# A list scheduler with other durations and loads, one choice for 20 units, and a first weight load behind the gathers, in a gated linear attention with a routed FFN

## The chip, the cores and the metric

One core of one Trainium2 chip. The metric is the device time of the whole kernel in microseconds (us). Before: 425.37 us, the median of 3 runs (424.46 to 426.98).

## The reference

Two stages, on one core, in float32:

```python
# attention: batch 4, 8 heads, 768 tokens, head size 48
for t in range(S):
    state = alpha[:, :, t, :, None] * state + np.einsum('bhd,bhe->bhde', k[:, :, t], v[:, :, t])
    y[:, :, t] = np.einsum('bhd,bhde->bhe', q[:, :, t], state)
...
# routed FFN: x is y laid out as 3072 tokens x 384, 8 experts, w1 384x1024, w2 1024x384
logits = x @ w_gate
order = np.argsort(-flat)            # all 3072*8 logits, largest first
for idx in order:
    tok, e = (int(idx) // E, int(idx) % E)
    if assigned[tok] >= 0 or counts[e] >= cap:   # cap = 384
        continue
    assigned[tok] = e
...
out[mask] = np.maximum(x[mask] @ w1[e], 0.0) @ w2[e]
```

So every token goes to one expert, each expert gets exactly 384 tokens, and who gets which depends on one global order of the logits.

## The kernel before

**Attention.** The sequence is cut into 6 chunks of 128 tokens; a unit is one chunk of one batch, all 8 heads, so there are 24 units (`unit(n)`, L352). A unit runs over all five engines:

- DVE: a scan over alpha (`sc`, L363), a reciprocal (L365), the keys scaled by it (`kh`, L373), a second scan (`ga`, L368), and the update of the carried state (`st`, L420 and L426).
- POOL: the queries scaled (`qh`, L378), the causal mask on the scores (`sm`, L407, two per unit), the carried state scaled (`ms`, L423).
- PE: transposed keys (L391), scores (L401), the state's increment (L415), outputs (L434: a part from the carried state, `qh` by `ms`, then a part from the chunk, `sm` by `vr`), the gate's logits (L457) and their transpose into one PSUM bank (L462, `lg`).
- ACT: evictions of PSUM (L394, L405, L451, L461).
- SP: the loads of alpha, k, q, v (L332).

**Choice.** `choice` (L468) takes the logits of a group of finished units. On DVE it copies them out of PSUM (L481), takes each token's largest logit (L484), turns it into digits (L490 to L107), marks the chosen expert (L498 to L502) and compares the first digit with 128 thresholds (`cmp`, L506, 128 elements per unit and partition). PE then counts per expert and threshold, one matmul per unit (L518). DVE adds the counts up (L529) and after the last group but one takes `need` (L534). In this kernel there are four groups: units 0 to 7, 8 to 15, 16 to 19, 20 to 23, each due as soon as its units are done (`at = n1 + 0.6`).

**Routing and FFN.** For each expert in turn, `round_` (L710) finds the threshold logit, digit by digit: five `level`s (L672), each a group of PE counts (L682), a row sum (L687), a DVE maximum (L690), then a compare on DVE (L699). Then it computes the indices of the 384 tokens (L834). Tokens are gathered from DRAM (`x_dram`, three indirect DMAs on POOL, L841), transposed (L913) and split in a high and a low part. An expert's weights come in `GP` = 4 pieces of 768 KB. Each piece is loaded once by POOL's queue (`hi`, L862), ACT writes its negative (two instructions, L872), and a second, accumulating DMA adds the full-precision weights to leave the remainder (`low`, L876). The FFN needs both: `ffn1` (L946) multiplies high by high, high by low and low by high, ACT and DVE split the hidden layer (L957, L959), `ffn2` (L977) does the second product, and the rows are scattered to the output (L991). Between attention and FFN the attention output, which lies transposed in SBUF, is transposed back and stored to `x_dram` (SP, L547, 24 stores): 8 units in the attention's own list, 16 after it (`rest`, L621).

**What sets the order.** Neither part is emitted as it is written. `op(...)` (L173) notes an operation with its engine, a duration in us, what it reads and writes, the PSUM banks it uses (`take`/`give` hold one for a chain of operations) and `at`, the time at which it is due. `plan()` (L193) is a list scheduler: it simulates the engines with these durations, and on each engine takes, of the operations that could start within 0.12 us of the earliest, the one with the smallest key:

```python
for o in reversed(ops):
    o.key = min([o.at] + [s.key for s in succ[o]])
...
t, o = min(((t, o) for t, o in c if t <= t0 + 0.12), key=lambda z: (z[1].key - z[1].boost, z[1].idx))
```

What comes out is the fixed order of the instructions on each engine; on the chip every engine works its own list off in order and waits where an input isn't there. There are two plans: one for attention with the choices (L580) and one for routing and FFN (L1020). `FIRST_HI` says how many `hi` pieces of expert 0, expert 1 and the others are issued as soon as the expert's number is known (L893); the others follow the gathers in `second` (L884).

Of the kernel before, what the change touches and what calls it, by code (L numbers as in the profile page):

```python
# [29 lines left out]
def gla_moe_kernel(ctx, tc, q, k, v, alpha, w_gate, w12, out):  # L30
# [4 lines left out]
    HP = H // 2  # L35
# [137 lines left out]
    def op(eng, dur, fn, r=(), w=(), banks=(), at=0.0, after=(), lat=LAT, take=None, give=None, follow=(), boost=0.0,  # L173
           dma=0.0, soft=(), small=False):
        o = Op()
        o.small = small
# [12 lines left out]
        o.pre = pre  # L189
        ops.append(o)  # L190
        return o

    def plan(begin=()):  # L193
# [7 lines left out]
        queue, again = {}, {}  # L201
        after_small = False
        todo = list(ops)
        out_ = []
        while todo:
# [121 lines left out]
    for i, (e, d_, f) in enumerate(LATE):  # L327
        lates.append(op(e, d_, f, after=lates[-1:], at=9.0 + 0.5 * i))


    def loads(n):
        r = RING  # L332
        sz = 1.25
        first = n == 0
        for nm, src, dst in (("al", alpha, AL), ("k", k, KR), ("q", q, QR), ("v", v, VR)):
            def fn(nm=nm, src=src, dst=dst):
                t = dst[n % r[nm]]
                if nm != "al":
# [7 lines left out]
            op("SP", sz if nm != "v" else 0.95, fn, w=[(nm, n)], at=n - 3.0, lat=2.2)  # L346


    def unit(n):
# [9 lines left out]
        for i, (lo, hi) in enumerate(parts):  # L359
# [23 lines left out]
            op("DVE", 1.26 / f, fore, r=[("al", n), ("sc", n)], w=[("ga", n)], at=n)  # L383
            op("DVE" if n == 0 else "POOL", 1.0 / f, scale_q, r=[("q", n), ("ga", n)], w=[("qh", n)], at=n + 0.1)
        if mid:
            t = [None]

            def keys():
                t[0] = xt([128, HP, C], 0)
                for p in range(HP):  # L390
                    P_.transpose(t[0][:, p], kh[:, p], ident)  # L391

            op("PE", 0.62, keys, r=[("kh", n)], w=[("T", n)], banks=("T",), at=n + 0.2, take="T")
            op("ACT", 0.6, lambda: A.activation(kn, t[0], AF.Copy), r=[("T", n)], w=[("kn", n)],  # L394
               banks=("T",), at=n + 0.3, give="T")
# [6 lines left out]

        op("PE", 1.15, scores, r=[("kh", n), ("qh", n)], w=[("S0", n), ("S1", n)], banks=("S0", "S1"), at=n + 0.3)
        for h in range(2):
            op("ACT", 0.6, lambda h=h: A.activation(sm[:, h], sps[:, h], AF.Copy), r=[(f"S{h}", n)],  # L405
               w=[("sm", n)], banks=(f"S{h}",), at=n + 0.4)
            op("POOL", 0.95, lambda h=h: G.affine_select(  # L407
                sm[:, h], sm[:, h], pattern=[[0, HP], [1, C]], compare_op=OP.is_ge, fill=0.0, base=0,
                channel_multiplier=-1), r=[("sm", n)], w=[("sm", n)], at=n + 0.5)
        if mid:  # L410
# [6 lines left out]

            op("PE", 0.62, states, r=[("kn", n), ("v", n), ("pads", 0)], w=[("KV", n)], banks=("KX",), at=n + 0.6)
            if c == 0:
                op("DVE", 0.3, lambda: V.tensor_copy(st_, kvp), r=[("KV", n)], w=[("st", n)], banks=("KX",),  # L420
                   at=n + 0.6)
        if c:
            op("POOL", 0.42, lambda: G.tensor_tensor(ms, st_, bc(total, D), op=OP.mult),  # L423
               r=[("sc", n), ("st", n - NBAT)], w=[("m", n)], at=n + 0.15)
# [3 lines left out]

        def outputs():
            fresh = set()  # L430

            def go(h, p, lhs, rhs, last):
                g, s = p % 2, p // 2
                P_.matmul(yv[64 * g:64 * g + D, h, s], lhs, rhs, start=(h, g) not in fresh, stop=last and s == 1,  # L434
                          skip_group_check=True)
                fresh.add((h, g))

            if c:
                for p in range(HP):
                    for h in range(2):  # L440
                        hs = slice(64 * h, 64 * h + D)
                        go(h, p, ms[hs, p], qh[hs, p], False)
# [4 lines left out]
        op("PE", (0.65 if c else 0) + 1.15, outputs,  # L447
           r=[("qh", n), ("v", n), ("sm", n), ("pads", 0)] + ([("m", n)] if c else []), w=[("Y", n)],
           banks=("Y",), at=n + 0.8)
        yt = YT[n]  # L450
        op("ACT", 0.62, lambda: A.activation(yt, yv, AF.Copy), r=[("Y", n)], w=[("yt", n)], banks=("Y",), at=n + 0.9)  # L451

        def logits():
# [5 lines left out]
        lt = LT[n % RING["lt"]]  # L459
        op("PE", 0.4, logits, r=[("yt", n), ("wg", 0)], w=[("LT", n)], banks=("KX",), at=n + 1.0)  # L460
        op("ACT", 0.3, lambda: A.activation(lt, ltp, AF.Copy), r=[("LT", n)], w=[("lt", n)], banks=("KX",), at=n + 1.0)  # L461
        op("PE", 0.25, lambda: P_.matmul(lgp[:, n % 8], lt, sel, start=True, stop=True), r=[("lt", n)],  # L462
           w=[("LG", n)], banks=("KX",), at=n + 1.1, after=lg_read.get(n // 8 - 1, ()))
# [5 lines left out]
    def choice(i, n0, n1):  # L469
        sl = slice(n0, n1)  # L470
        m_ = n1 - n0
        lw = L[:, sl]
        at = n1 + 0.6 if n1 < NU else NU - 0.2
        tl = {}

        def tile_(nm, shape, dt=F32):
            tl[nm] = ap_.tile(shape, dt, name=f"{nm}_{i}")
            return tl[nm]

        def c0():  # L480
            V.tensor_copy(lw, lgp[:, n0 % 8:n0 % 8 + m_])  # L481

# [37 lines left out]

        x = op("PE", 0.06 * m_ + 0.1, counts, after=[x], banks=("KX",), at=at)

# [13 lines left out]

    done = []
    GROUPS = ((0, 8), (8, 16), (16, 20), (20, 24))

# [9 lines left out]
    for n in range(NU):  # L549
        loads(n)  # L550
        unit(n)
        for i, (n0, n1) in enumerate(GROUPS):
            if n1 == n + 1:
                choice(i, n0, n1)
    ev = []
    for n in range(Y_IN_ATTENTION):
# [9 lines left out]
        if wide:  # L566
            xo = op("PE", 0.31, lambda tr=tr: tr(0), r=[("yt", n)], after=lastw["sm", NU - 1], banks=("S0", "S1"),
                    at=40.0 + n, take=f"s{wide}")
            xo = op("PE", 0.31, lambda tr=tr: tr(1), after=[xo], banks=("S0", "S1"), at=40.0 + n)
            ev.append(op("ACT", 0.6, lambda n=n, t=t: y_evict(n, t[0]), after=[xo], banks=("S0", "S1"),  # L570
                         at=40.0 + n, give=f"s{wide}"))
        else:
            xo = op("PE", 0.31, lambda tr=tr: tr(0), r=[("yt", n)], after=lastw["S0", Y_FROM], banks=("T",),
                    at=40.0 + n, take="T")
            xo = op("PE", 0.31, lambda tr=tr: tr(1), after=[xo], banks=("T",), at=40.0 + n)
            ev.append(op("ACT", 0.6, lambda n=n, t=t: y_evict(n, t[0]), after=[xo], banks=("T",), at=40.0 + n,
# [494 lines left out]
```

## Time and profile before

| | |
|---|---|
| median of 3 runs | 425.37 us (424.46 to 426.98) |
| profiled execution | 424.8 us, its span 423.2 us, mean granted TensorE clock 0.953 |
| PE busy | 388.3 us (92% of the span), 4166 matmuls |
| DVE busy | 266.8 us (63%) |
| POOL busy | 186.5 us (44%) |
| ACT busy | 173.9 us (41%) |
| DMA | 88.85 MB, 210 GB/s over the span |
| attention, until its last `lg` | 128 us |
| routing of expert 0, gathers, first weights | 128 to 168 us |
| FFN with the other experts' routing beside it | from 163.5 us to the end |

PE is busy nearly all the time, but a busy share of 92% is a mean over three stages. The time is lost where PE is idle or runs at a lower granted clock, and that is in the first 190 us. An engine's order is fixed, so an idle PE waits for one named instruction. "PEclk" is the granted TensorE clock: 1.0 is 2.4 GHz, 0.5 is 1.2 GHz, and a mean between them is a stretch that has some of each.

### The profile page before, as it was taken

How to read it: one execution, taken by the hardware profiler on the slowest of the kernel's cores; microseconds unless marked ns; L12 is line 12 of the kernel's file. 1: busy time of each engine (PE TensorE's matmuls, PEld its weight loads, DVE VectorE, ACT ScalarE, POOL GpSimd, SP SyncE). 2: the span in 40 equal slices, each digit the busy share in tenths (PEclk: the TensorE clock that was granted, in tenths of full speed). 3: DMA queues.
4: the chain of work that ended last, by engine and by line, in shares of the span. 5: the costliest groups of instructions: out<-in, count | busy, mean ns of one | idle time of the engine just before them, and what ended most of it. 6: DMA issues, size and time to landing. Idle time of an engine off the chain costs nothing.

```text
span 423.2 us, 10477 instructions
## 1 busy us (share of the span) xinstructions
PE 388.3 (92%) x4166; PEld 343.5 (81%) x4166; DVE 266.8 (63%) x673; ACT 173.9 (41%) x320; POOL 186.5 (44%) x271
## 2 busy tenths in 40 slices
PE   6789979998888858999999999999999999999991
PEld 3667768787666846898998999999999999999990
DVE  8798898879915746686685866766766754131110
ACT  4355535554535412434326263263262263453210
POOL 9667648785810033151454372352253283430302
PEclk8699989999989688899999999999999999999997
DMA  7986756663015559999899999899899899999201
GB/s 224 390 305 211 225 166 213 203 219 103 5 37 191 172 164 249 218 263 226 219 289 265 228 354 192 198 315 189 190 324 181 171 377 196 293 298 199 79 2 57
DMA packets 30178, 88.85 MB, mean 210 GB/s; under 512 B 4144, under 2 KB 10544, under 8 KB 30128
## 3 DMA queue, kind: packets, MB, share of 16 engines
q0 software_dynamic: 12288, 59.78, 55.4%
q1 hardware_dynamic: 17840, 28.39, 20.2%
q8 instruction: 33, 0.54, 0.5%
q14 instruction: 17, 0.14, 0.1%
HBM read 78.72 MB, written 9.44 MB: 208 GB/s over the span
## 4 chain that ended last, share of the span: by engine, by line
PE 66%; DVE 13%; issue 8%; POOL 5%; DMA 5%; ACT 1%; POOLq 0%; DVEq 0%; ACTq 0%
PE h L946 19%; PE y L977 18%; PE y L434 6%; PE xt L682 6%; DMA wset<-in_w_dram 5%; PE s L401 4%; PE xt L391 2%; PE xt L913 2%; PE xt L457 2%; DVE sc L363 2%; PE xt L415 2%; POOL out_dram L991 1%; DVE kh L373 1%; DVE ga L368 1%; PE xt L830 1%
## 5 line engine op out<-in xcount | busy, mean ns | idle before, releaser
L977 PE MATMUL y<-wset,hh 128*128 128x384 f32 x384 | 101.9, 346 | 0.0
L946 PE MATMUL h<-xh,wset 128*128 128x384 f32 x384 | 91.1, 346 | 2.1 <-DMA wset<-in_w_dram 1.9
L957 ACT ACTIVATE hh<-h 128x384 fp32r<-128x384 f32 x64 | 31.2, 488 | 111.8 <-PE h L946 101.8
L959 DVE SCALAR_TENSOR_TENSOR hl<-h,hh 128x384 fp32r<-128x384 f32 x64 | 35.5, 554 | 61.2 <-ACT hh L957 61.1
L946 PEld LDWEIGHTS h<-xh,wset 128*128 128x128 f32 x384 | 68.1, 191 | 3.3 <-DMA wset<-in_w_dram 2.4
L977 PEld LDWEIGHTS y<-wset,hh 128*128 128x128 f32 x384 | 67.2, 189 | 0.0
L977 PE MATMUL y<-wset,hl 128*128 128x384 f32 x192 | 64.7, 337 | 0.0
L872 ACT ACTIVATE wset<-wset 128x768 fp32r<-128x768 f32 x64 | 51.2, 839 | 25.9 <-DMA wset<-in_w_dram 25.8
L862 POOL DMA_DIRECT2D wset<-in_w_dram x32 | 22.2, 720 | 82.8 <-DVE m L749 34.8
L876 POOL DMA_DIRECT2D wset<-in_w_dram x32 | 30.5, 1167 | 34.1 <-ACT wset L872 33.3
L946 PE MATMUL h<-xl,wset 128*128 128x384 f32 x192 | 45.2, 343 | 0.0
L841 POOL DMA_INDIRECT xr<-x_dram,idx x24 | 25.2, 1049 | 37.6 <-DVE idx L834 15.3
L991 POOL DMA_INDIRECT out_dram<-yo,idx x24 | 26.2, 1090 | 35.2 <-ACT yo L985 29.3
L407 POOL TENSOR_SCALAR_AFFINE_SELECT sm<-sm 128x512 f32<-128x512 f32 x48 | 31.1, 668 | 19.6 <-ACT sm L405 11.8
L682 PEld LDWEIGHTS <-cmp 128*128 128x128 bf16 x816 | 30.2, 118 | 8.5 <-DVE cmp L699 4.4
L378 POOL TENSOR_TENSOR qh<-qr,ga 128x512 f32<-128x512 f32 x23 | 32.0, 1391 | 10.4 <-DVE ga L368 7.8
L977 PEld LDWEIGHTS y<-wset,hl 128*128 128x128 f32 x192 | 36.0, 188 | 0.0
L405 ACT ACTIVATE sm<-s 128x512 f32<-128x512 f32 x48 | 26.7, 596 | 18.6 <-PE s L401 17.7
L946 PEld LDWEIGHTS h<-xl,wset 128*128 128x128 f32 x192 | 33.7, 189 | 0.2
L699 DVE TENSOR_TENSOR cmp<-nd,iota 128x1536 bf16<-128x1536 bf16 (+2 forms) x32 | 32.7, 1032 | 0.9
L368 DVE TENSOR_TENSOR_SCAN ga<-al,d 128x516 f32<-128x516 f32 (+1 forms) x25 | 29.6, 1184 | 2.0
L434 PE MATMUL y<-sm,vr 128*48 128x128 f32 x384 | 28.0, 292 | 2.8 <-POOL sm L407 2.8
(161 smaller groups left out, 598.0 us busy)
## 6 DMA issues: line engine op xcount, KB each, us to landing
wset<-in_w_dram POOLq DMA_DIRECT2D x64, 768.0 KB, 9.1
kr<-in_k_dram SPq DMA_DIRECT2D x24, 256.0 KB, 4.4
qr<-in_q_dram SPq DMA_DIRECT2D x24, 256.0 KB, 4.4
al<-in_alpha_dram SPq DMA_DIRECT2D x23, 258.5 KB, 3.9
vr<-in_v_dram SPq DMA_DIRECT2D x24, 192.0 KB, 3.6
x_dram<-xga SPq DMA_DIRECT2D x24, 192.0 KB, 1.9
xr<-x_dram,idx POOLq DMA_INDIRECT x24, 4.7
out_dram<-yo,idx POOLq DMA_INDIRECT x24, 6.2
```

What stands on the lines that cost most here:

```text
L368: V.tensor_tensor_scan(ga[:, lo:hi], a[:, lo:hi], dps[:, lo:hi], 1.0, op0=OP.mult, op1=OP.add)
L378: (V if n == 0 else G).tensor_mul(qh[:, ps_], qr[:, ps_], ga[:, lo:hi].rearrange("p (g x) -> p g x", x=C1)[:, :, 1:])
L407: op("POOL", 0.95, lambda h=h: G.affine_select(sm[:, h], sm[:, h], pattern=[[0, HP], [1, C]], compare_op=OP.is_ge, fill=0.0, base=0, chann ...
L434: P_.matmul(yv[64 * g:64 * g + D, h, s], lhs, rhs, start=(h, g) not in fresh, stop=last and s == 1, skip_group_check=True)
L682: P_.matmul(rt_c, cmp_[:, j // U, :, j % U], o[:, j], start=j == 0, stop=j == NU - 1, skip_group_check=True)
L699: x = op("DVE", (1.75 if nt == 128 else 0.95) / n + 0.03, lambda js=js: V.tensor_tensor(words(cbuf[t % 2], nt, js), keyed(d, nt, js), each ...
L872: pre.append(op("ACT", 0.84, lambda hs=hs: A.activation(WS[i % 2][:, 1, g][:, hs], WS[i % 2][:, 0, g][:, hs].bitcast(F32), AF.Copy, scale= ...
L876: accs[i, g] = op("POOL", 0.92, lambda: nc.gpsimd.dma_start(WS[i % 2][:, 1, g], w12.bitcast(F32R)[bass.ds(eng_reg[i], 1), :, g].rearrange( ...
L946: P_.matmul(o, WS[i % 2][:, a, g, c0 + d * 128:c0 + (d + 1) * 128], x[:, d], start=m_ == 0 and d == 0, stop=m_ == 2 and d == DB - 1)
L957: a_ = op("ACT", 0.49, lambda: A.activation(HHT[m], o, AF.Relu), after=[y], r=[("hb", n_)], w=[("hh", n_)], at=at, boost=25, lat=0.1)
L959: op("DVE", 0.54, lambda: V.scalar_tensor_tensor(HLT[m], o, 0.0, HHT[m], op0=OP.max, op1=OP.subtract), after=[a_], r=[("hb", n_), ("hh", n ...
L977: P_.matmul(YB[b][:, :Dm], a[:, bs], w, start=q == 0 and n == 0, stop=q == FB - 1 and n == 2)
```

## The change

1. **Durations and shapes in the attention's plan.** Many durations are other numbers (scores 1.15 to 0.9, key transposes 0.62 to 0.44, masks 0.95 to 0.65, `qh` 1.0 to 1.3, loads 1.25 to 0.9). Each PE operation carries a shape; a change of shape costs 0.13 or 0.2 us in the plan, and the same shape as the one before is preferred by 0.4. The outputs become two operations (`carried_` and `within`) that hold the bank Y together. Four DVE constants (`LATE`, the tables `iotas` for the digits 2 to 5) are due at 40.0, so behind everything else, in place of 16.5 to 18. Back-transposes (Y) of units 0 to 2 use the bank of the key transposes and have no lower limit (`Y_FROM` gone, `Y_WIDE` 5 to 3).
2. **One choice for 20 units.** `GROUPS` has two entries, and the first is due at `CHOICE` = 23.15. The copies of the logits out of PSUM stay apart (`logits_out`, four groups as before).
3. **First weights behind the gathers.** `FIRST_HI` for expert 0 is 0 and `second(0)` issues all four pieces behind the three gathers.

```diff
-Y_WIDE = 5
-Y_FROM = 19
+Y_WIDE = 3
+SAME, CHOICE = 0.4, 23.15
...
-FIRST_HI = (1, 2, 4)
+FIRST_HI = (0, 2, 4)
...
-                t, o = min(((t, o) for t, o in c if t <= t0 + 0.12), key=lambda z: (z[1].key - z[1].boost, z[1].idx))
+                t, o = min(((t, o) for t, o in c if t <= t0 + 0.12), key=lambda z: (
+                    z[1].key - z[1].boost - SAME * (z[1].shape == last_shape is not None), z[1].idx))
...
+                o.dur += (0.13 if o.shape != 64 else 0.2) * (o.shape != last_shape)
+                last_shape = o.shape
...
-        lates.append(op(e, d_, f, after=lates[-1:], at=9.0 + 0.5 * i))
+        lates.append(op(e, d_, f, after=lates[-1:], at=9.0 + 0.5 * i if e == "POOL" else 40.0))
...
-        sz = 1.25
+        sz = 0.9
...
-        op("PE", 1.15, scores, r=[("kh", n), ("qh", n)], w=[("S0", n), ("S1", n)], banks=("S0", "S1"), at=n + 0.3)
+        op("PE", 0.9, scores, shape=64, r=[("kh", n), ("qh", n)], w=[("S0", n), ("S1", n)], banks=("S0", "S1"), at=n + 0.3)
...
-        at = n1 + 0.6 if n1 < NU else NU - 0.2
+        at = CHOICE if n1 < NU else NU - 0.2
...
-    GROUPS = ((0, 8), (8, 16), (16, 20), (20, 24))
+    GROUPS = ((0, 20), (20, 24))
+
+    def logits_out(n0, n1):
+        x = op("DVE", 0.18, lambda: V.tensor_copy(L[:, n0:n1], lgp[:, n0 % 8:n0 % 8 + n1 - n0]),
+               r=[("LG", n) for n in range(n0, n1)], banks=("KX",), at=n1 + 0.1, after=inits + copied[-1:])
+        lg_read[n0 // 8] = lg_read.get(n0 // 8, ()) + (x,)
+        copied.append(x)
...
-            for g in range(1, GP):
+            for g in range(GP):
                 hi(g, [x], rows)
-                low(g - 1, [his[0, g]])
-                rows = [accs[0, g - 1]]
+                rows = [his[0, g]]
+                if g:
+                    low(g - 1, rows)
+                    rows = [accs[0, g - 1]]
```

Two places in the order of the instructions. The first is DVE at the end of attention; `kh` is the scaled key of unit 23, `m` to `cmp` are the choice, L the logits' copy. Before:

```order
L368 SCALAR_TENSOR_TENSOR ga_143<-al_121,d 128x516
L481 COPY L<-xt_168 128x32
L484 TENSOR_REDUCE m_2_1544<-L 128x4
L487 TENSOR_TENSOR val_2_1547<-L,m_2_1544 128x32
...
L502 TENSOR_TENSOR o_100<-ramp_b,chu_99 128x32
L506 TENSOR_TENSOR cmp_2_1584<-dig_98,iota 128x512
L373 TENSOR_TENSOR kh_146<-kr_126,sc_141 128x512
L529 TENSOR_TENSOR cnt<-cnt,xt_168 128x8
L534 TENSOR_SCALAR need<-cnt 128x8
L481 COPY L<-xt_168 128x32
```

and now:

```order
L371 SCALAR_TENSOR_TENSOR ga_143<-al_121,d 128x516
L429 TENSOR_TENSOR st_160<-ms_155,xt_168 128x192
L376 TENSOR_TENSOR kh_146<-kr_126,sc_141 128x512
L544 COPY L<-xt_168 128x32
L487 TENSOR_REDUCE m_0_1499<-L 128x20
L490 TENSOR_TENSOR val_0_1502<-L,m_0_1499 128x160
...
L505 TENSOR_TENSOR o_100<-ramp_b,chu_99 128x160
L509 TENSOR_TENSOR cmp_0_1540<-dig_98,iota 128x2560
L530 COPY cnt<-xt_168 128x8
```

The last `kh` stood behind a choice of 4 units and stands ahead of one of 20. The choices of units 0 to 7 and 8 to 15, which stood between the scans of units 10 and 11 and of units 19 and 20, are gone from there. The four `iotas` have moved: three stood behind the scan of unit 1 and one behind that of unit 2, and now they stand behind the scans of units 20, 21 and 23. On PE, the 20 counts of the new choice stand behind the `lg` of unit 21; between the `lg` of unit 19 (the last logits that the choice needs) and the counts PE has two whole units of scores, logits, outputs and `lg`.

The second place is POOL from the first expert's number (`ei`) on; `wset` is a weight piece, L862 and L875 load high parts, L876 and L889 accumulate low ones, wset_1746 and wset_1709 are expert 0's, wset_2190 and wset_2154 expert 1's. Before:

```order
L857 TENSOR_LOAD ei_1762
...
L862 DMA wset_1746<-in_w_dram 128x1536
L841 DMA xr_1747<-x_dram,idx_1825 128x384 x3
...
L862 DMA wset_1746<-in_w_dram 128x1536
...
L876 DMA wset_1746<-in_w_dram 128x1536
...
L857 TENSOR_LOAD ei_1763
```

and now:

```order
L870 TENSOR_LOAD ei_1725
...
L854 DMA xr_1710<-x_dram,idx_1788 128x384 x3
...
L875 DMA wset_1709<-in_w_dram 128x1536
...
L875 DMA wset_1709<-in_w_dram 128x1536
...
L889 DMA wset_1709<-in_w_dram 128x1536
...
L870 TENSOR_LOAD ei_1726
...
L875 DMA wset_2154<-in_w_dram 128x1536
...
L889 DMA wset_1709<-in_w_dram 128x1536
```

The first `hi` has moved from ahead of the three gathers to behind them, and expert 1's first `hi` (wset_2154) now stands ahead of expert 0's third and fourth `low`, where both of its first pieces stood ahead of the fourth `low` alone.

## Rows read from the trace of the kernel before

**Rows 1.** The page: 40 slices of granted TensorE clock, in tenths.
```profile
PEclk8699989999989688899999999999999999999997
```
**Rows 2.** Busy time by stretch: PE, PEld, DVE, ACT, POOL (count), PEclk, DMA share, GB/s.
```profile
58.00:63.00 5.00, 5.00 (x60) 4.06 (x59) 4.89 (x8) 1.19 (x2) 2.06 (x2) 0.66 0.47 151
63.00:99.00 36.00, 36.00 (x644) 28.33 (x641) 30.52 (x51) 20.19 (x42) 26.15 (x32) 1.00 0.69 220
117.00:121.00 4.00, 3.70 (x46) 2.76 (x46) 1.08 (x4) 0.00 (x0) 0.00 (x0) 0.57 0.00 0
191.00:386.00 195.00, 194.74 (x1709) 183.85 (x1710) 117.85 (x353) 81.83 (x141) 78.28 (x105) 1.00 0.97 249
```
**Rows 3.** Timeline around the first choice: start, us, engine, line, operation [idle before].
```profile
53.38 0.22 DVE L481 COPY L<-xt 128x64 f32<-128x64 f32 x1
56.91 0.68 DVE L506 TENSOR_TENSOR cmp<-dig,iota 128x1024 bf16<-128x1024 bf16 x1
55.85 0.39 PE L462 MATMUL xt<-sel,lt 128*128 128x8 f32 x2 [0.56 <-ACT lt L461]
57.91 0.40 PE L518 MATMUL xt<-o,cmp 128*128 128x8 bf16 x8 [1.67 <-DVE st L426]
```
**Rows 4.** Timeline of PE around the second choice.
```profile
104.49 0.56 PE L415 MATMUL xt<-vr,kn 128*48 128x48 f32 x16 [1.04 <-ACT yta L451]
104.99 1.16 PE L401 MATMUL s<-qh,kh 64*128 64x128 f32 x16
108.03 0.39 PE L462 MATMUL xt<-sel,lt 128*128 128x8 f32 x2
```
**Rows 5.** Timeline around the third choice, PE and DVE, and the last `lg`.
```profile
113.52 0.43 PE L457 MATMUL xt<-yta,wg 128*32 128x128 f32 x8 [0.64 <-DVE L L481]
117.16 0.68 DVE L373 TENSOR_TENSOR kh<-kr,sc 128x512 f32<-128x512 f32 x1
117.30 0.30 PE L518 MATMUL xt<-o,cmp 128*128 128x8 bf16 x4 [1.44 <-DVE cmp L506]
128.23 0.39 PE L462 MATMUL xt<-sel,lt 128*128 128x8 f32 x2
```
**Rows 6.** Timeline of DVE in the routing: the same instruction on 24 units.
```profile
149.41 0.35 DVE L766 TENSOR_TENSOR val<-L,m 128x192 bf16<-128x192 f32 x1
```
**Rows 7.** Groups of lines, 0 to 120 us: count | busy us, mean ns | idle before.
```profile
L321 DVE TENSOR_SCALAR iota<-iota 128x256 bf16<-128x256 bf16 (+1 forms) x4 | 2.6, 680 | 0.0
```
**Rows 8.** Waits, 0 to 120 us: who waited for whom: us, times, longest us.
```profile
PE xt L391 <- DVE kh L373: 2.7, 4, 1.6
```
**Rows 9.** Timeline of DVE and POOL around the first gathers.
```profile
149.68 0.15 DVE L834 TENSOR_SCALAR idx<-xt 128x3 int32<-128x3 f32 x1
146.18 0.76 POOL L862 DMA_DIRECT2D wset<-in_w_dram  x1 [21.55 <-DMA x_dram<-xga]
154.70 1.06 POOL L841 DMA_INDIRECT xr<-x_dram,idx  x1 [7.76 <-DVE g L685]
158.29 0.61 POOL L862 DMA_DIRECT2D wset<-in_w_dram  x1
```
**Rows 10.** One tile: stores to `x_dram`, 120 to 165 us.
```profile
DMA to landing us min/median/max: 1.8/1.9/6.0
```
**Rows 11.** One line: the `hi` loads (L862), 140 to 200 us.
```profile
DMA to landing us min/median/max: 6.0/8.6/14.6
```
**Rows 12.** The chain of waits, two of its DMAs: start, us, what.
```profile
158.86 9.22 DMA wset<-in_w_dram
179.86 10.97 DMA wset<-in_w_dram
```
**Rows 13.** Timeline of PE: the FFN's first matmuls, and a wait for weights.
```profile
163.52 0.76 PE L946 MATMUL h<-xh,wset 128*128 128x384 f32 x3
168.13 2.05 PE L946 MATMUL h<-xh,wset 128*128 128x384 f32 x6 [1.33 <-DMA wset<-in_w_dram]
```
**Rows 14.** The page: the costliest group of ACT's copies for the low parts.
```profile
L872 ACT ACTIVATE wset<-wset 128x768 fp32r<-128x768 f32 x64 | 51.2, 839 | 25.9 <-DMA wset<-in_w_dram 25.8
```

More of the change, by code (lines that the diff above doesn't have):

```diff
@@ L173, in op @@
     def op(eng, dur, fn, r=(), w=(), banks=(), at=0.0, after=(), lat=LAT, take=None, give=None, follow=(), boost=0.0,
-           dma=0.0, soft=(), small=False):
+           dma=0.0, soft=(), small=False, shape=None):
         o = Op()
-        o.small = small
+        o.small, o.shape = small, shape
         o.take, o.give, o.follow, o.boost, o.dma, o.soft = take, give, follow, boost, dma, soft
@@ L383, in unit @@
             op("DVE", 1.26 / f, fore, r=[("al", n), ("sc", n)], w=[("ga", n)], at=n)
-            op("DVE" if n == 0 else "POOL", 1.0 / f, scale_q, r=[("q", n), ("ga", n)], w=[("qh", n)], at=n + 0.1)
+            op("DVE" if n == 0 else "POOL", 1.3 / f, scale_q, r=[("q", n), ("ga", n)], w=[("qh", n)], at=n + 0.1)
         if mid:
@@ L391, in keys @@
                     P_.transpose(t[0][:, p], kh[:, p], ident)
-            op("PE", 0.62, keys, r=[("kh", n)], w=[("T", n)], banks=("T",), at=n + 0.2, take="T")
+            op("PE", 0.44, keys, shape=128, r=[("kh", n)], w=[("T", n)], banks=("T",), at=n + 0.2, take="T")
             op("ACT", 0.6, lambda: A.activation(kn, t[0], AF.Copy), r=[("T", n)], w=[("kn", n)],
@@ L427, in unit, with carried_, go, within @@
                    w=[("st", n)], banks=("KX",), at=n + 0.6)
[L429 to L442, printed above, removed]
+        fresh = set()
+        def carried_():
+            for p in range(HP):
+                for h in range(2):
+                    hs = slice(64 * h, 64 * h + D)
+                    go(h, p, ms[hs, p], qh[hs, p], False)
+        def go(h, p, lhs, rhs, last):
+            g, s = p % 2, p // 2
+            P_.matmul(yv[64 * g:64 * g + D, h, s], lhs, rhs, start=(h, g) not in fresh, stop=last and s == 1,
+                      skip_group_check=True)
+            fresh.add((h, g))
+        def within():
             for h in range(2):
@@ L445, in outputs @@
                     go(h, p, vr[:, 4 * (p // 2) + 2 * h + p % 2], sm[:, h, p], True)
-        op("PE", (0.65 if c else 0) + 1.15, outputs,
-           r=[("qh", n), ("v", n), ("sm", n), ("pads", 0)] + ([("m", n)] if c else []), w=[("Y", n)],
-           banks=("Y",), at=n + 0.8)
+        if c:
+            op("PE", 0.45, carried_, shape=4848, r=[("qh", n), ("m", n), ("pads", 0)], w=[("Y", n)], banks=("Y",),
+               at=n + 0.75, take="Y")
+        op("PE", 0.9, within, shape=48, r=[("v", n), ("sm", n), ("pads", 0)] + ([("Y", n)] if c else []),
+           w=[("Y", n)], banks=("Y",), at=n + 0.8, take=None if c else "Y")
         yt = YT[n]
-        op("ACT", 0.62, lambda: A.activation(yt, yv, AF.Copy), r=[("Y", n)], w=[("yt", n)], banks=("Y",), at=n + 0.9)
+        op("ACT", 0.62, lambda: A.activation(yt, yv, AF.Copy), r=[("Y", n)], w=[("yt", n)], banks=("Y",), at=n + 0.9, give="Y")
         def logits():
@@ L459, in unit @@
         lt = LT[n % RING["lt"]]
-        op("PE", 0.4, logits, r=[("yt", n), ("wg", 0)], w=[("LT", n)], banks=("KX",), at=n + 1.0)
+        op("PE", 0.23, logits, shape=32, r=[("yt", n), ("wg", 0)], w=[("LT", n)], banks=("KX",), at=n + 1.0)
         op("ACT", 0.3, lambda: A.activation(lt, ltp, AF.Copy), r=[("LT", n)], w=[("lt", n)], banks=("KX",), at=n + 1.0)
-        op("PE", 0.25, lambda: P_.matmul(lgp[:, n % 8], lt, sel, start=True, stop=True), r=[("lt", n)],
+        op("PE", 0.15, shape=128, fn=lambda: P_.matmul(lgp[:, n % 8], lt, sel, start=True, stop=True), r=[("lt", n)],
            w=[("LG", n)], banks=("KX",), at=n + 1.1, after=lg_read.get(n // 8 - 1, ()))
@@ L506, in c7 @@
             V.tensor_tensor(CM[i], keyed(dig0[:, 0], T, sl), each(iota, T, sl), op=OP.is_ge)
-        x = op("DVE", 0.18, c0, r=[("LG", n) for n in range(n0, n1)], banks=("KX",), at=at, after=inits)
-        lg_read[n0 // 8] = lg_read.get(n0 // 8, ()) + (x,)
-        for d_, f in ((0.18, c1), (0.45, c2), (0.32, c3), (0.5, c4), (0.6, c5), (0.2, c6), (0.13 * m_, c7)):
+        x = copied[-1]
+        for d_, f in ((0.1 + 0.01 * m_, c1), (0.1 + 0.01 * m_, c2), (0.3, c3), (0.5 + 0.01 * m_, c4), (0.35 + 0.01 * m_, c5),
+                      (0.15 + 0.006 * m_, c6), (0.04 + 0.073 * m_, c7)):
             x = op("DVE", d_, f, after=[x], at=at)
@@ L519, in counts @@
                           skip_group_check=True)
-        x = op("PE", 0.06 * m_ + 0.1, counts, after=[x], banks=("KX",), at=at)
+        x = op("PE", 0.034 * m_, counts, shape=128, after=[x], banks=("KX",), at=at)
         def add():
@@ L551, in gla_moe_kernel @@
         unit(n)
+        for n0, n1 in ((0, 8), (8, 16), (16, 20), (20, 24)):
+            if n1 == n + 1:
+                logits_out(n0, n1)
         for i, (n0, n1) in enumerate(GROUPS):
```

22 lines of the change are left out of this document (10 added, 12 removed).

## Prediction

> **What bounds the kernel now.** I read the page first. Its row of granted clock [rows 1] stands near full almost everywhere, with dips in the slices around 60, 120, 140 and 160 us (a slice is 10.6 us). So PE is the engine to watch, and the losses have places. The busy times by stretch [rows 2] say what these places are. From 63 to 99 us, in the middle of attention, PE is busy 36.00 of 36.00 us at clock 1.00: there PE itself is the bound, and nothing that the other engines do costs anything. From 191 to 386 us the FFN is busy 194.74 of 195.00 us at 1.00: there too. Whatever this change gains must therefore come from before 63 us, from 99 to 128 us, or from 128 to 191 us.
>
> The timeline shows who holds PE up in these stretches. In the first [rows 3], DVE takes the choice of units 0 to 7 from 53.38 us, with its own `kh` queued behind. PE waits 0.56 us at 55.85 (ACT could not evict while the copy had the bank) and 1.67 us at 57.91. That second wait is put down to `st`, but it stands at the counts, and the `cmp` in front of it ended only at 57.6. Behind these gaps the clock is 0.66 from 58 to 63 us [rows 2]. The second choice shows the same less strongly: 1.04 us at 104.49 [rows 4]. The third is worst [rows 5]: 0.64 us at 113.52, 1.44 us at 117.30 for the counts, and `kh` of unit 23 could only run at 117.16, behind the choice. The clock behind it is 0.57 from 117 to 121 us [rows 2]. The last `lg` of attention starts at 128.23.
>
> After attention, the indices of the first gather are ready at 149.83, but POOL issues it at 154.70 [rows 9]. What lies between are stores to `x_dram`: normally they land after 1.9 us, the slowest after 6.0 [rows 10]. The first weight load was issued at 146.18, among the last stores.
>
> **The sum.** It is made against the profiled execution, 424.8 us; the median of the runs is 0.6 above it, and I add that at the end.
>
> *Choices in the middle of attention, gone or moved.* A gap counts whole, since PE is the bound around it; a stretch of lower clock counts as its length times what is missing from 1.00.
> - First choice: 0.56 + 1.67 [rows 3] + 5.00 x (1 - 0.66) = 1.7 [rows 2]: -3.9 us.
> - Second choice: -1.0 us [rows 4].
> - Third choice: 0.64 + 1.44 [rows 5] + 4.00 x (1 - 0.57) = 1.7 [rows 2]: -3.8 us.
>
> Together -8.7 us. The copies of the logits stay, 0.22 us each [rows 3], and the PE counts stay in number; both are paid now.
>
> *The choice of 20 at the end.* DVE works the choice of 8 units from 53.38 to 56.91 in eleven small instructions, 3.53 us, then `cmp`, 0.68 us for 1024 elements [rows 3]. For 20 units `cmp` has 2560: 1.7 us. The small ones I leave as they are, because the same `val` instruction on 24 units takes 0.35 us [rows 6]: they are fixed cost. So 5.2 us. What hides it is PE's work between the `lg` of unit 19 and the counts, two units of scores, logits, outputs and `lg`; one unit is 3.4 us (104.99 to the end of the `lg` at 108.42, [rows 4]), so 6.8 us. The four `iotas`, 2.6 us in all [rows 7], now stand in front of it on DVE, and 5.2 + 2.6 = 7.8 us would show by 1.0; if DVE leads PE there, by nothing. I take +0.5. If only one unit of cover is left, 7.8 - 3.4 = 4.4 us are uncovered, and the lower clock behind a gap, 1.7 as above, comes on top. Bounds: 0 to +6.1.
>
> *The `iotas` leave the start.* Their 2.6 us [rows 7] stood behind the scans of units 1 and 2, with `kh` of the next unit queued after them. PE waited for `kh` 2.7 us in 4 waits, the longest 1.6 [rows 8]. I take that one wait as theirs, -1.5. Bounds: 0 (the loads are the limit there) to -2.6.
>
> *Durations, shapes, separate outputs, loads, early Y of unit 0.* These only reorder. PE's groups change shape 141 times in attention where it was 145. The trace has no price for a change; the small `lg` group, two matmuls of 8 columns, takes 0.39 us with everything in it [rows 4], so four changes are worth 0 to -1.6. Where PE is full the order of full groups changes nothing: I take 0. The transposes of unit 0 are moved, not added.
>
> *First weights behind the gathers.* Without the load among them I expect the last stores to land like the others, 6.0 - 1.9 = 4.1 us earlier [rows 10], so the gathers go at 150.6, soon after the indices (149.83). What do the weights do? The first `hi` is then issued where the second was, 158.29 - 4.1 = 154.2 [rows 9], and with the shortest landing of such a load, 6.0 us [rows 11], it is there at 160.2, ahead of the FFN's first matmul at 163.52 [rows 13]. But the stream is what ends this stage. The chain goes through the first `low`, 9.22 us from 158.86, for which PE waits 1.33 us, and through the last, 10.97 us from 179.86 [rows 12, 13]; from 191 us PE does not stop. From 158.29 to 190.83 the queue lands the same nine pieces, 3.6 us each, and now it has to land the first `hi` in the same stretch as well: -4.1 + 3.6 = -0.5 us. I take that. Bounds: -3.3 if the FFN can start as soon as its first `hi` is there (160.2 for 163.52). On the other side the first `low` must wait for that `hi` and ACT's two copies of 0.84 us [rows 14], 160.2 + 1.7 = 161.9, where it was issued at 158.86: +3.0.
>
> The Trainium skill speaks against this part: its page DMA: Bandwidth & Descriptors, section Rules for kernel authors, says to issue a DMA early, compute, and wait for it late. Rows 9 and 10 show the other side, an early load with six-microsecond stores beside it; by the rule alone this part would be worth the +3.0 of rival 2. The same page's section Anatomy of one DMA gives 2.0 us plus bytes by 436 GB/s, an estimate of 3.8 us for 768 KB, and by it this term would be 2.2 us lower; no load here came under 6.0 [rows 11], and the row decides.
>
> Sum: -8.7 + 0.5 - 1.5 - 0.5 = -10.2 us, so 414.6 for a profiled execution, and with 0.6 a median of **415.2 us**. All bounds at their best: -8.7 - 2.6 - 1.6 - 3.3 = -16.2, 409.2 us. All at their worst: -8.7 + 6.1 + 3.0 = +0.4, 425.8 us.
>
> **Rivals.**
>
> 1. *The choice of 20 isn't covered.* PE works in order, so logits and outputs of units 22 and 23 queue behind the 20 counts, and everything after attention behind those. For it: in the third choice just this wait of PE for `cmp` is there [rows 5]. Against it: that choice stood ahead of the last `kh`, this one stands behind it. Price: +6.1 for +0.5: 420.8 us.
> 2. *The first expert's weights are late.* The `hi` stands behind the gathers, the `low` behind it, and expert 1's first piece ahead of the third `low`. For it: PE already waits for the first `low` [rows 13], so any delay of it shows. Against it: the gathers come 4.1 us earlier. Price: +3.0 for -0.5: 418.7 us.
> 3. *Slower: the new order has a hole, and the clock stays down.* The plan is built on other durations, so a bank held too long or an input that comes late by the chip's time makes gaps in each unit. Behind the gaps of rows 3 and 5 the clock went towards its 1.2 GHz level. A unit's 3.4 us of work [rows 4] then takes another 3.4. It decides from four units on: 415.2 + 4 x 3.4 = 428.8 us, slower than before. Against it: in the full stretch of rows 2 there was slack on every other engine (DVE busy 30.5 of 36, POOL 26.2).
> 4. *Nothing is gained.* The choice's gaps go, but PE had to wait there for scans or loads in any case, and the waits appear elsewhere: 425.4 us. Against it: from 63 us on PE was full without any choice beside it [rows 2].
>
> **How the numbers follow.** Forecast 0.60, rival 1 0.15, rival 2 0.13, rival 3 0.06, rival 4 0.06. A measurement of this kernel can tell about 0.5% from no change, 2.1 us (its three runs spread over 2.5). The forecast and rivals 1 and 2 lie beyond that: faster 0.88, same 0.06 (rival 4), slower 0.06 (rival 3). The range runs from 409.5, nearly all bounds at their best, to 421.5, just beyond rival 1; what it leaves out is rivals 3 and 4 and sums of rivals 1 and 2.
>
> **What would show it.** In the changed profile: PE without gaps of over 0.5 us between 50 and 118 us, clock 1.00 from 58 to 63 us and at 100 to 118; the last `lg` about 10 us earlier, near 118; a wait of at most 1 us at the counts of 20; slowest store to `x_dram` near 2 us, first gather within 1 us of its indices; the first `low` still what PE waits for, about 10 us earlier than 168.1. It would be wrong if the last `lg` came at 122 or later (rival 1, or 3 with low clock over many slices), or if attention gained its 9 us and the first long stretch of `h` matmuls still began after 161 (rival 2).

## The result and the profile after

The changed kernel takes 414.6 us (median of 4 runs, 411.77 to 415.02), the kernel before 424.94 beside it (424.46 to 426.98); the ratio is 0.9746, with a 95% interval of 0.9709 to 0.9783. In all ratios and intervals a run of over 1.5% above the fastest of its kernel is left out as slow (414.76 in the first experiment, and one of the kernel before on two of the chips); medians and spreads hold every run. 415.2 us was forecast. The total was met, but two terms of the sum missed by a lot and in opposite directions, and that is what the experiments are about.

The profiled execution has a span of 413.0 us where it was 423.2. Set beside each other, the marks of the two traces say where the 10.2 us come from. Each row is the start of an instruction, but for the indices, where it is the end.

| mark | before | after | difference |
|---|---|---|---|
| last `lg` of attention | 128.23 | 115.07 | -13.2 |
| indices of the first gather ready | 149.83 | 136.73 | -13.1 |
| first gather issued | 154.70 | 137.99 | -16.7 |
| PE goes on with the first low part | 168.13 | 156.35 | -11.8 |
| end of the span | 423.2 | 413.0 | -10.2 |

Attention gained more than forecast (-9.7 with the iotas and the late choice). The gathers gained 3.6 more, near the 4.1 forecast. Then 6.5 us were given back in the weights, 2.9 more than the gathers gained.

The busy times by stretch (columns as in [rows 2]), the last stretch the FFN's:

```profile
58.00:63.00 5.00, 5.00 (x100) 4.34 (x98) 4.63 (x6) 3.43 (x7) 4.20 (x6) 1.00 0.73 250
63.00:99.00 36.00, 36.00 (x662) 29.13 (x660) 34.31 (x52) 20.32 (x42) 24.77 (x33) 1.00 0.62 198
103.00:115.50 12.50, 12.50 (x214) 9.83 (x208) 5.56 (x15) 6.43 (x14) 4.99 (x8) 1.00 0.02 5
180.00:375.00 195.00, 194.88 (x1717) 184.60 (x1716) 118.92 (x354) 80.84 (x140) 78.11 (x104) 1.00 0.96 247
```

The clock from 58 to 63 us is 1.00 where it was 0.66, and PE has no gap from 30 us to the end of attention. The FFN is as it was. The choice of 20, in the timeline of DVE and PE:

```profile
103.94 0.19 DVE L544 COPY L<-xt 128x32 f32<-128x32 f32 x1 [4.83 <-PE xt L468]
104.52 0.44 DVE L490 TENSOR_TENSOR val<-L,m 128x160 bf16<-128x160 f32 x1
107.96 1.48 DVE L509 TENSOR_TENSOR cmp<-dig,iota 128x2560 bf16<-128x2560 bf16 x1
...
110.24 0.39 PE L468 MATMUL xt<-sel,lt 128*128 128x8 f32 x2
110.48 0.80 PE L521 MATMUL xt<-o,cmp 128*128 128x8 bf16 x20
```

DVE even waits 4.83 us for PE's `lg` of unit 19; the choice ends at 109.44, PE comes to the counts at 110.48 and doesn't wait. From the indices on, the timeline of POOL and PE:

```profile
137.99 1.17 POOL L854 DMA_INDIRECT xr<-x_dram,idx  x1 [27.47 <-DVE dig L786]
142.22 1.19 POOL L875 DMA_DIRECT2D wset<-in_w_dram  x2
149.18 0.92 POOL L889 DMA_DIRECT2D wset<-in_w_dram  x1 [5.77 <-ACT wset L885]
...
163.26 0.54 POOL L875 DMA_DIRECT2D wset<-in_w_dram  x1 [10.84 <-DVE m L762]
163.91 0.89 POOL L889 DMA_DIRECT2D wset<-in_w_dram  x1
...
156.35 1.30 PE L961 MATMUL h<-xh,wset 128*128 128x384 f32 x3 [2.80 <-DMA wset<-in_w_dram]
172.82 1.16 PE L961 MATMUL h<-xh,wset 128*128 128x384 f32 x3 [1.82 <-DMA wset<-in_w_dram]
```

The gathers are within 1.3 us of their indices (4.9 in [rows 8, 9]). But the first low part is issued 11.2 us behind the first gather (149.18 to 137.99), where it was 4.2 [rows 9, 12], and PE waits 2.80 us for it (and 1.05 us before that for the first `hi`, at 147.36). The third low part stands behind POOL's reading of expert 1's number, for which POOL idles 10.84 us; PE waits 1.82 us for it. Of that place the prediction named expert 1's load, and not the reading in front of it.

### The profile page after: what moved, and what is told of

Its sections match the earlier page's. It is cut to its first block, busy times and chain, and to the rows that moved or that the text cites. A ratio compares the mean times of both kernels' runs of the same rounds, so it can differ in the third digit from the quotient of the medians.

```text
span 413.0 us, 10416 instructions
## 1 busy us (share of the span) xinstructions
PE 383.0 (93%) x4166; PEld 341.1 (83%) x4166; DVE 258.3 (63%) x649; ACT 173.5 (42%) x320; POOL 186.1 (45%) x271
## 4 chain that ended last, share of the span: by engine, by line
PE 74%; issue 8%; POOL 5%; DVE 5%; DMA 4%; ACT 1%; POOLq 0%; ACTq 0%
PE h L961 20%; PE y L992 20%; PE y L442 9%; PE s L404 6%; PE xt L695 6%; DMA wset<-in_w_dram 4%; PE xt L394 2%; PE xt L418 2%; PE xt L463 2%; PE xt L928 2%; PE xt L468 2%; POOL out_dram L1006 1%; PE xt L843 1%; POOL cmp L322 1%; DVE hot L837 1%
## 5 line engine op out<-in xcount | busy, mean ns | idle before, releaser
L961 PE MATMUL h<-xh,wset 128*128 128x384 f32 x384 | 92.3, 350 | 5.7 <-DMA wset<-in_w_dram 5.7
L992 PEld LDWEIGHTS y<-wset,hh 128*128 128x128 f32 x384 | 68.2, 191 | 0.0
L875 POOL DMA_DIRECT2D wset<-in_w_dram x32 | 21.0, 670 | 67.7 <-PE h L961 39.6
L889 POOL DMA_DIRECT2D wset<-in_w_dram x32 | 29.7, 1154 | 40.5 <-ACT wset L885 39.6
L410 POOL TENSOR_SCALAR_AFFINE_SELECT sm<-sm 128x512 f32<-128x512 f32 x48 | 32.9, 702 | 19.8 <-ACT sm L408 16.6
L1006 POOL DMA_INDIRECT out_dram<-yo,idx x24 | 27.2, 1134 | 30.5 <-ACT yo L1000 22.1
L695 PEld LDWEIGHTS <-cmp 128*128 128x128 bf16 x816 | 30.2, 118 | 10.2 <-DVE cmp L712 5.8
L381 POOL TENSOR_TENSOR qh<-qr,ga 128x512 f32<-128x512 f32 x23 | 29.8, 1295 | 4.8 <-issue 1.8
L695 PE MATMUL xt<-oc,cmp 128*128 128x8 bf16 x720 | 28.9, 175 | 2.3 <-DVE cmp L712 2.3
L442 PE MATMUL y<-sm,vr 128*48 128x128 f32 x384 | 26.8, 283 | 4.0 <-POOL sm L410 4.0
```

The source lines that it names most:

```text
L381: (V if n == 0 else G).tensor_mul(qh[:, ps_], qr[:, ps_], ga[:, lo:hi].rearrange("p (g x) -> p g x", x=C1)[:, :, 1:])
L410: op("POOL", 0.65, lambda h=h: G.affine_select(sm[:, h], sm[:, h], pattern=[[0, HP], [1, C]], compare_op=OP.is_ge, fill=0.0, base=0, chann ...
L695: P_.matmul(rt_c, cmp_[:, j // U, :, j % U], o[:, j], start=j == 0, stop=j == NU - 1, skip_group_check=True)
L889: accs[i, g] = op("POOL", 0.92, lambda: nc.gpsimd.dma_start(WS[i % 2][:, 1, g], w12.bitcast(F32R)[bass.ds(eng_reg[i], 1), :, g].rearrange( ...
L961: P_.matmul(o, WS[i % 2][:, a, g, c0 + d * 128:c0 + (d + 1) * 128], x[:, d], start=m_ == 0 and d == 0, stop=m_ == 2 and d == DB - 1)
L992: P_.matmul(YB[b][:, :Dm], a[:, bs], w, start=q == 0 and n == 0, stop=q == FB - 1 and n == 2)
```

## The experiments

**Which part is worth what.** The change has three separable parts: the plan (durations, shapes, loads, late iotas), the choice of 20, and the weight order. Four kernels with one or two parts:

*The old weight order in the changed kernel.*
```diff
-FIRST_HI = (0, 2, 4)
+FIRST_HI = (1, 2, 4)
...
-            for g in range(GP):
+            for g in range(1, GP):
                 hi(g, [x], rows)
-                rows = [his[0, g]]
-                if g:
-                    low(g - 1, rows)
-                    rows = [accs[0, g - 1]]
+                low(g - 1, [his[0, g]])
+                rows = [accs[0, g - 1]]
```


> The changed kernel with the weight order of before: the first hi load ahead of the three gathers. Its total was 414.6 us. Theory: the new weight order costs time, since from the indices on the changed kernel gains 3.7 us at the first gather (4.9 us late before, 1.2 now) but loses 4.8 between the first gather and the landing of the first low part (13.4 before, 18.2 now) and 1.7 behind it, +2.8 in all; then this kernel takes 411.8 us, PE's waits for weights fall from 5.7 us to about 2, and the slowest store to x_dram takes about 6 us again. Rival (the prediction's -0.5 for this part, the lost time having another cause): 415.1 us or more.

Measured: 408.73 us (406.8 to 414.76), ratio 0.9608 (0.9546 to 0.9671). The new weight order costs some 6 us here, twice the 2.9 that the marks gave, and the kernel without it beats both. In the two traces 1.2 us of this lie ahead of the weights, in attention, whose order both kernels share (last `lg` at 113.78 for 115.07, indices at 135.56 for 136.73), and 4.5 between the indices and PE's first low part (150.71 for 156.35). PE's waits for weights are 2.35 and 0.75. The expected slow stores didn't come back: of the last stores the slowest lands after 2.6 us. Why is told below.

*The new weight order in the kernel before* (the same edit the other way round).

> The kernel before with only its weight order changed. Theory (the new order costs 2.8 us): 427.7 us. Rival (the prediction's term, -0.5): 424.4 us. Both: the gathers start within 1.5 us of their indices.

Measured: 428.81 us, ratio 1.0096 (1.0059 to 1.0132): slower by 1%. The gathers go at 150.91, 3.8 us earlier, near what was forecast, and still the end is later. Its timeline:

```profile
169.09 1.30 PE L948 MATMUL h<-xh,wset 128*128 128x384 f32 x3 [1.99 <-DMA wset<-in_w_dram]
186.69 0.79 PE L948 MATMUL h<-xh,wset 128*128 128x384 f32 x3 [2.97 <-DMA wset<-in_w_dram]
```

and its busy time by stretch:

```profile
155.00:175.00 20.00, 14.17 (x140) 11.54 (x139) 10.22 (x29) 7.03 (x11) 4.38 (x7) 0.66 0.87 232
```

PE goes on 1.0 us later than before (169.09 for 168.13), then waits 2.97 us for the third low part, where its one wait from 175 us on was 0.61, and has a clock of 0.66 from 155 to 175 us where the kernel before has 0.75 over the same window.

*The old choices in the changed kernel.*
```diff
-    GROUPS = ((0, 20), (20, 24))
+    GROUPS = ((0, 8), (8, 16), (16, 20), (20, 24))
...
-        at = CHOICE if n1 < NU else NU - 0.2
+        at = n1 + 0.6 if n1 < NU else NU - 0.2
```


> The changed kernel with the four choices of before (8, 8, 4 and 4 units, each due as its units are done); the durations, shapes, loads and weights stay changed. Theory: attention's gain of 13.2 us (last lg 128.2 to 115.1) is 8.7 from the gaps at the choices, as the prediction had it, and some 4.5 from the durations and shapes; then the gaps come back and this takes 423.3 us, with its last lg near 124. Rival 1: the gaps came from the wrong durations of the plan, and with the measured ones a choice of 8 is hidden too: 414.6 to 416. Rival 2: the choices are worth all of the 13.2: 427.8.

Measured: 416.79 us, ratio 0.9824 (0.9774 to 0.9875); last `lg` at 117.49. Rival 1 is the nearest: with the new plan the old choices cost some 2 us and not 8.7.

*The new choice in the kernel before* (`GROUPS`, `CHOICE`, `logits_out`).

> The kernel before with only the choice changed (one for 20 units, due at 23.15, copies of the logits apart); durations, shapes, loads and weights as before. Theory (8.7 us are the choice's): 416.2 us, last lg near 119.5. Rival 1 (the durations did it): 424.9. Rival 2 (all 13.2 are the choice's): 411.7.

Measured: 420.13 us, ratio 0.9889 (0.9842 to 0.9936); last `lg` at 122.18. Between the theory and rival 1.

*The new plan alone* (both edits above).

> The changed kernel with the four choices and the weight order of before, so with the new durations, shapes, loads and late iotas alone. If the parts add up as the single runs show (choice_old 416.8, and the weight order worth 3.4 us in the kernel before and 5.9 in the changed one): 410.9 to 413.4 us, alone 12 to 14.5 us below the kernel before.

Measured: 415.81 us, ratio 0.9785 (0.9737 to 0.9833). Above what was expected: the parts don't add up. All together, each beside the median of the kernel before on the same chip:

| plan | choice of 20 | new weight order | us | before beside it | difference |
|---|---|---|---|---|---|
| | | x | 428.81 | 425.37 | +3.4 |
| | x | | 420.13 | 425.37 | -5.2 |
| x | | | 415.81 | 424.99 | -9.2 |
| x | | x | 416.79 | 425.37 | -8.6 |
| x | x | | 408.73 | 425.37 | -16.6 |
| x | x | x | 414.6 | 424.94 | -10.3 |

By the last column the plan is worth -9.2 alone; the choice -5.2 alone and -7.4 behind the plan; the weight order +3.4 alone, +0.6 behind the plan (the intervals overlap) and +6.3 behind both. The -7.4 isn't the choice's own work alone: by the marks of these two traces 4.5 us are gained in attention (last `lg` at 118.31 and 113.78), and 3.5 at the first gather (5.0 and 1.5 us behind its indices).

**Why the weight order's price varies.** Two of these kernels have the same old weight order, but different ends of attention. The timeline of POOL and DVE in the kernel with the plan alone:

```profile
136.20 0.76 POOL L875 DMA_DIRECT2D wset<-in_w_dram  x1 [22.48 <-DVE offs L763]
139.73 0.15 DVE L847 TENSOR_SCALAR idx<-xt 128x3 int32<-128x3 f32 x1
144.84 1.06 POOL L854 DMA_INDIRECT xr<-x_dram,idx  x1 [7.88 <-DVE g L698]
```

and the view of one tile there, `x_dram`, whose first line ends with the start of the first store and of the last:

```profile
L557 SPq DMA_DIRECT2D x_dram<-xga x23: 319/320/402, 114.8 to 137.7; - x23
DMA to landing us min/median/max: 1.8/1.9/6.1
```

The same two views of the kernel with plan and choice, the second only to 136.9 us, since the view of a tile counts the gathers' landings in and one of those, 3.3 us, is longer than any of the last stores':

```profile
134.73 0.76 POOL L875 DMA_DIRECT2D wset<-in_w_dram  x1 [25.50 <-DVE hot L837]
135.40 0.15 DVE L847 TENSOR_SCALAR idx<-xt 128x3 int32<-128x3 f32 x1
137.04 1.16 POOL L854 DMA_INDIRECT xr<-x_dram,idx  x1 [1.55 <-DVE chu L787]
```

```profile
L557 SPq DMA_DIRECT2D x_dram<-xga x23: 319/320/624, 113.3 to 133.6; - x23
DMA to landing us min/median/max: 1.8/1.9/2.6
```

With the plan alone the last store is issued at 137.7, behind the load at 136.20; it lands after 6.1 us and the gather is 5.0 us late. With the choice of 20 as well the last store is at 133.6, ahead of the load at 134.73: no slow store, the gather 1.5 us behind its indices. The other kernels with the old order fall on the same two sides: before, load 146.18 and last store 147.7, slowest landing 6.0; choice alone, 140.40 and 143.0, 6.1; the new load lengths alone (below), 145.64 and 148.0, 6.5. So in the kernel with plan and choice the very collision that the new weight order is there to avoid is gone, and what is left of the new order is its cost.

That plan and choice order it away doesn't follow, though. Measured from the first expert's number (`ei`, written at 134.24 with the plan alone and at 129.91 with both), the last store comes after 3.5 and 3.7 us, so it didn't move; the load comes after 2.0 and 4.8. The view of the load's line has the step in front of it on POOL, with the plan alone and with both:

```profile
L875 POOLq MOVE wset<-in_w_dram x1: 29/29/29, 135.5 to 135.5; - x1
L875 POOLq MOVE wset<-in_w_dram x1: 29/29/29, 131.3 to 131.3; - x1
```

From this step to the load it is 0.7 us in the four kernels with the collision, and 3.4 us here. Issued after 0.7 us, at 132.0 by this estimate, this load too would have stood among the last stores. In two more kernels with plan, choice and an early first load (the last two of this section) POOL pauses in the same place, for 2.9 and 3.3 us. In all three pauses, and in none of the four short steps, the trace has one packet of instructions on DMA queue q14. That POOL waits for its instructions there is likely, but not shown: each of these is one profiled execution, and no run moves that packet alone.

**What in the plan does it.**

*The old load lengths in the changed kernel* (one number for alpha, k and q, one for v).
```diff
-        sz = 0.9
+        sz = 1.25
...
-            op("SP", sz if nm != "v" else 0.7, fn, w=[(nm, n)], at=n - 3.0, lat=2.2)
+            op("SP", sz if nm != "v" else 0.95, fn, w=[(nm, n)], at=n - 3.0, lat=2.2)
```


> The changed kernel planned with the load lengths of before (1.25 and 0.95 us). The plan then believes DVE idle at the start, so the iotas come back behind the scans of units 1 and 2. Theory 1 (the load lengths are what gave DVE its early lead, 2 to 3 us of it at units 5 to 10 before, 4.5 to 9 now): 418 to 420 us, PE idle over 1.5 us between 20 and 50 us. Theory 2 (only the iotas move): the same as with the iotas at the start. Theory 3 (the other durations give the lead): 414.6.

Measured: 427.75 us, ratio 1.0052 (1.0017 to 1.0087), last `lg` at 125.70. Two numbers that are never executed give back all of the gain, more than any theory had. Its busy time by stretch:

```profile
50.00:110.00 60.00, 56.05 (x1020) 45.40 (x1018) 46.88 (x70) 32.69 (x68) 42.59 (x54) 1.00 0.59 186
```

and its timeline, the scaled key and the scores of unit 10 and a late wait:

```profile
55.66 0.67 DVE L376 TENSOR_TENSOR kh<-kr,sc 128x512 f32<-128x512 f32 x1
57.44 1.16 PE L404 MATMUL s<-qh,kh 64*128 64x128 f32 x16
117.33 2.08 PE L404 MATMUL s<-qh,kh 64*128 64x128 f32 x16 [3.17 <-POOL qh L381]
```

The same two views of the changed kernel:

```profile
50.00:110.00 60.00, 60.00 (x1084) 48.72 (x1080) 51.49 (x80) 34.44 (x71) 43.45 (x58) 1.00 0.52 169
```

```profile
47.17 0.67 DVE L376 TENSOR_TENSOR kh<-kr,sc 128x512 f32<-128x512 f32 x1
56.86 1.16 PE L404 MATMUL s<-qh,kh 64*128 64x128 f32 x16
```

10.6 of the 13.2 us that attention had gained are gone. What differs, and is the likely cause, is DVE's lead over PE: the scaled key of unit 10 is done 9.0 us ahead of its scores in the changed kernel (47.84 to 56.86) and 1.1 us with the old load lengths (56.33 to 57.44); in the kernel before it is 3.0 at units 9 and 10, where a choice of 8 takes DVE 4.2 us [rows 3]. In the plan, a unit's four loads took 3 x 1.25 + 0.95 = 4.70 us, more than PE's seven groups with the new durations (3.43, and at most 0.98 for their shapes), so the plan took the loads for the bound and had no reason to let DVE run ahead. On the chip the loads are issued about 2.6 us per unit (alpha of consecutive units at 11.79, 14.38 and 16.93 us in the changed kernel), so the plan was waiting for nothing.

*The new load lengths in the kernel before* (the same edit the other way round).

> The kernel before with only the load lengths of its plan changed (0.9 and 0.7 in place of 1.25 and 0.95). Theory (four loads of a unit take 4.70 us in the old plan against 4.84 of PE, so the plan lets DVE run no further ahead of PE than the loads allow; with 3.40 it does): DVE's lead reaches 5 us or more before the first choice, most of the gaps at the choices go, 413 to 418 us. Rival (the measured durations of PE, DVE and POOL are needed too): 422 to 425.

Measured: 426.34 us, ratio 1.0038 (1.0005 to 1.0071): the theory falls. The lead is there (6.8 us at unit 10), but PE waits elsewhere (the view of waits, 20 to 120 us: who for whom, us, times, longest):

```profile
PE xt L462 <- DVE st L426: 4.5, 4, 1.9
PE xt L518 <- DVE st L426: 2.2, 2, 1.5
PE xt L518 <- DVE cmp L506: 1.1, 1, 1.1
```

PE waits for the state updates on DVE, which share a bank with the logits; that they stand behind scans that run too far ahead is likely, but not shown. A lead alone isn't enough; the loads and the other durations were both needed. Which of the others matter wasn't tried.

*No shapes in the plan* (`SAME` 0, and 0.1 us for every operation in place of a price for a change).

> The changed kernel planned with no price for a change of PE tile shape and no preference for the same one (each operation 0.1 longer in the plan, the iotas fall behind the scan of unit 23). Theory 1 (shapes matter: a group followed by one of its own shape takes 0.07 to 0.1 us less, about 0.1 per unit over 20 units): 416.6 us. Theory 2 (the prediction's 0): 414.6. Theory 3 (the shapes make most of the durations' 10 us): over 420.

Measured: 417.6 us, ratio 0.9843 (0.9774 to 0.9912), last `lg` at 116.40. On the side of theory 1: 3.0 us over the changed kernel by the medians, though the intervals just touch. In the trace attention ends 1.3 us behind the latest of the five kernels that share the changed attention (113.78 to 115.07).

*The iotas at the start* (forced between the second scan and the scaled key of unit 1).

> The changed kernel with the four iotas forced between the scans of unit 1 and its scaled key on DVE. Theory (DVE's early lead over PE is what carries the later gain): their 2.6 us show in full, last lg 117.7, 417.2 us. Rival (the start is limited by loads and by the first mask, PE has 4.0 us of waiting at 13 us in any case): 414.6. The prediction's term was 1.5: 416.1.

Measured: 415.49 us, ratio 0.9791 (0.9711 to 0.9872), last `lg` at 114.53. Nothing that the runs can tell from the changed kernel: the rival.

**Can the weights be better still?** Three orders around the first expert. *The third low part ahead of the reading of expert 1's number, in the changed kernel* (`follow=[accs[0, 2]]` on that read).

> The changed kernel, but expert 0's third low part is issued ahead of the reading of expert 1's number on POOL, as it was before; the first hi load stays behind the gathers. Theory A (POOL waits 10.8 us for that number with the low part queued behind, and PE then 1.8 us for the low part): 411.5 to 412.8 us. Theory B (what costs is the late first hi load, 142.2 us in place of 134.7 with the old order, and this kernel doesn't move it): 414.6, with PE's wait of 2.8 us for the first low part unchanged.

Measured: 412.41 us, ratio 0.9709 (0.9644 to 0.9774). The wait at 172.82 is gone from the trace, as theory A has it, and 1.86 us for the first low part stay, nearer to B; in the total the interval overlaps the changed kernel's, so a gain isn't shown. The profiled execution is the slowest of the five (415.14, the others 411.16 to 412.6): in it the last store takes 4.0 us with no weight load issued before it lands, and the first gather is 4.4 us behind its indices, where the changed kernel has 1.3. So a load isn't the only thing that can hold up the last store; what did here stays open.

*The first low part ahead of the second hi load, in the kernel with the old weight order.*

> The changed kernel with the weight order of before, and in it the first low part ahead of the second hi load. Theory (the first low part takes 9.1 us since two hi loads share the queues with it, and PE waits 2.35 us for it): the low lands in 6 to 7 us, PE's wait goes, 406.5 us. Rival (the second hi then comes later, and PE waits there): 408.7.

Measured: 412.52 us, ratio 0.9711 (0.9646 to 0.9776): worse. PE waits 0.46 us for the first, but the next low part is issued at 154.15, and PE waits 2.00 us at 161.37. From 150 to 170 us PE is busy 14.42 us, where the kernel with the old weight order has 19.29 at the same clock (0.83): the rival, and more than it had.

*The last low part ahead of the reading, in the kernel with the old weight order.*

> The changed kernel with the weight order of before, and the last low part of expert 0 ahead of the reading of expert 1's number. Theory (PE waits 0.75 us for that part, issued behind two of expert 1's hi loads): 408.0. Rival (expert 1's loads come later by what this one comes earlier): 408.7 or more.

Measured: 408.8 us, ratio 0.9607 (0.9532 to 0.9682): no change against 408.73. The best kernel of the study is the changed one with the old weight order.

## Why the prediction came out right, and which steps failed

- *PE is the bound, the losses have places.* Right. The gaps and low clocks of [rows 2 to 5] are gone.
- *Choices, -8.7.* The gaps went, but they weren't the choice's alone. The new choice is worth 5.2 us by itself, and the plan with the four old choices left in it also loses most gaps: in the kernel with the plan alone PE waits 0.67, 0.78 and 0.55 us between 50 and 118 us, and the clock from 58 to 63 us is 1.00. The step that failed is "a gap counts whole": a gap needs a choice and a DVE with too little lead, and either part of the change removes most of it. One of the gaps was read wrongly besides: at 55.85 it wasn't the copy that kept ACT from evicting, for that had ended at 53.60; ACT was busy with the two `sm` of a unit until 55.5.
- *Durations, shapes, loads, 0 (0 to -1.6).* The worst step. "Where PE is full the order of full groups changes nothing" looked at 36 us of the kernel, and priced the shapes only. The plan is worth -9.2 alone. What it seems to set is how far DVE runs ahead, and with that whether an interruption reaches PE; the leads of the traces fit this, but with the new load lengths alone the lead was there and the gain wasn't.
- *Iotas, -1.5.* Not seen: 0.9 us by the medians, inside the spread of the runs. The bound 0 was the right one.
- *Choice of 20, +0.5.* It showed no wait; the 6.8 us of cover held (4.83 us of slack on DVE besides). `cmp` took 1.48 for 1.7.
- *Weights, -0.5 (-3.3 to +3.0).* Its first half came true in the kernel before: with this part alone the gathers go 3.8 us earlier. In the changed kernel there was nothing to gain there, since with the old order too the gather is 1.5 us behind its indices (1.3 with the new one). Its second half failed: +3.4 alone and +6.3 in the changed kernel, outside its bounds. The step that failed is "-4.1 + 3.6", which let the count of the stream's pieces decide. What decided was when PE has its first low part: that is issued 11.2 us behind the first gather for 4.2, just as the working of the +3.0 bound has it (161.9 for gathers at 150.6). Nor did the sum have that POOL would issue the third low part only behind expert 1's number, or the lower clock behind PE's longer waits (0.66 for 0.75 with this part alone). Late first weights were rival 2, and with it the Trainium skill's rule in DMA: Bandwidth & Descriptors, section Rules for kernel authors, to issue a DMA early. The runs agree with that rule here: +3.4 and +6.3 us for issuing it late.
- *The total.* 415.2 for 414.6 because attention gave 3.5 us more than forecast (-13.2 for -9.7) and the weights took back what the forecast hadn't, and the two nearly cancel. That it came within 0.6 us is luck; a right total doesn't make the terms right.

## What to carry to other kernels

In a list scheduler a duration isn't a description but an instruction: one resource that the plan thinks is the bound, here loads of 4.70 us per unit that took 2.6, shapes the emitted order of every other engine. Changing those lengths back cost 13 us here. Look for it in how far one engine runs ahead of the next, unit by unit, and not only at idle time. And a repair against a collision should be run again without itself once the rest of the change is in, for the collision may be gone. Then look at what took it away: here the stores stood where they did, and POOL's load was late by a pause that nobody planned.

## What the runs showed of the hardware

One load of 768 KB issued between the last stores to DRAM made the slowest of them land after 6.0 to 6.5 us (four kernels); issued 0.4 to 1.1 us behind the last store it didn't, 2.3 to 2.8 us (three kernels). One last store without any load beside it took 4.0 us. POOL paused 2.9 to 3.4 us between two steps of one DMA issue in three kernels, with a packet of instructions in the pause, where it took 0.7 in four others. A group of matmuls took less when the next had its shape: `sm` by `vr` at full clock 0.91 us of pace ahead of the state's increment (from its start to the next group's start, 3 cases, 63 to 99 us of the changed kernel), and 1.01 ahead of others.
